# A mixture-of-experts kernel in Winograd form: second-layer products in alternating groups of two

## The chip, the core and the metric

One NeuronCore of a Trainium2 chip runs the whole program. The metric is device time in microseconds (us) of one execution, median of several runs.

## The reference, cut to what matters

```python
x = attention(q, packed(k, v, p))             # 4 batches x 576 tokens, 8 heads of 64
x = moe_ref(x, w_in, w_out)                   # h = x @ w_in; (h * cos(h)) @ w_out
P = sinkhorn(exp(x @ w_gate))                 # 2304 tokens, 8 experts
out = np.zeros((N, D))
for e in range(E):                            # 8 experts, 512 -> 1024 -> 512
    h = np.maximum(x @ w1[e], 0.0)
    out += P[:, e:e + 1] * (h @ w2[e])
```

All of it is fp32. The change concerns the last loop, which takes nearly four fifths of the time.

## The kernel before, in words

The first part (attention, then the cosine layer) runs for about 390 us from orders written out by hand; the change leaves it alone except for the last few operations that prepare the second part.

The expert part is split into 16 units (half an expert each, `u` from 4 to 19) of three steps (`j`, 768 tokens each), so 48 steps. A step computes a first layer (x times w1, called G1 here, matmuls on line 758) and the second layer (h times w2, G2, line 849) of the step before. Each layer is a 2 by 2 block product in Winograd's form: seven products instead of eight, of 12 matmuls with 384 columns each (three matmuls per fp32 product, from a high and a low part of both factors). So a step has 14 products. The names `m` in `MULTS`, `WIDE` and `NARROW` number the products.

All eight PSUM banks are one tile, `bank`. G1 works in two pairs of banks, X and Y (`two_banks`), which exchange their parts from step to step; G2 accumulates its seven products in two chains, in banks 4, 5 and 6, 7 (`WIDE`), or, while bank 7 is needed for the gate's logits and normalisation or for output tiles, in banks 4, 5 and 6 alone (`NARROW`). The engines beside TensorE do the rest:

- ScalarE (ACT) makes copies between the bank pairs and casts the high parts: L741 of h, L710 of w1, L242 of w2, L665 of x.
- VectorE (DVE) makes the low parts of h (L742), adds G2's sums into the accumulator `acc` (L869), applies relu and the gate's scale (L770), and forms the sums of h (L813, L828, L831).
- GpSimd (POOL) makes the low parts of the weights and their sums (L711, L714, L243, L246).
- SyncE issues all loads.

The order on each engine is the order in which the Python code issues (`manual_schedule`); a queue is served strictly from its front. In the loop over `n` a step issues, seven times, one G1 product, an evacuation, one split of an h sum (`h_steps`), and one G2 product (`g2_step`):

```python
for n in range(7):
    step_side()
    next(steps)                  # G1 product n
    if prev is not None:
        h_steps(s - 1, n + 7)    # split of an h sum
    ...
    next(steps)                  # its evacuation
    if prev is not None:
        g2_step(*prev, n, narrow, pair_no)
```

`step_side` issues the gate's logits (L928, L932, L935) and its normalisation piece by piece in the first steps. In the first unit the slots of x are computed on the way (`x_steps`); later they are loaded, four slots in turn. `w1_make` and `t_make` are generators whose steps prepare the weights of the next unit. `scale_first` (L907) multiplies the accumulator by the first expert's gate once, in three steps of the third unit. `out_tile` (L913 to L916) transposes finished tiles in a bank, copies them out and stores them.

Of the kernel before, what the change touches and what calls it, by code (L numbers as in the profile page):

```python
# [8 lines left out]
F32 = mybir.dt.float32  # L9
# [5 lines left out]
ALU = mybir.AluOpType  # L15
# [19 lines left out]
MULTS = (0, 5, 1, 6, 4, 3, 2)  # L35
# [69 lines left out]
def tile_kernel(ctx: ExitStack, tc: tile.TileContext, qT, kT, v, pT, w_in, w_out, w_gate, w1, w2, out):  # L105
# [129 lines left out]
    def t_make(u):  # L235
# [13 lines left out]
        put(1, b11)  # L249
        yield  # L250
        comb(b11, b12, b11)
        put(5, b11)
        yield
        comb(b11, b22, b11)
        put(6, b11)
        yield
        put(3, b22)
        yield
        comb(b12, b22, b12)
        put(7, b12)  # L260
        yield
        put(2, b21)
        yield
        comb(b21, b21, b11)
# [425 lines left out]
    def w1_make(u, places):  # L690
# [28 lines left out]
        yield  # L719
        comb(s2, s1, a11, ALU.subtract)  # L720
        put(5, s2)
        yield
        put(1, a12)
        yield
        comb(a11, a11, a21, ALU.subtract)
        put(6, a11)
        yield
        comb(a12, a12, s2, ALU.subtract)
        put(4, s1)
# [44 lines left out]
    def g1_steps(u, j):  # L774
        s = NJ * u + j
        x = counts["chunk"] % 2
        counts["chunk"] += 1
        X, Y = two_banks(x), two_banks(1 - x)
        r22, r11, r21, r12, rs = (halves(t) for t in (raws[s % 2], *raws[2:6]))
        b = halves(base)  # L780

        g1_mult(u, 0, x, True)
        if u == U1 and j == 0:
            wh = w_slot(w1_slots[u][0])[0]
            for p in range(2):
                nc.tensor.matmul(
                    bank[:, 2 * (1 - x) + p, 0:HT], lhsT=wh[:, 0, 0:P], rhs=x_slot(0)[0][:, 0, :],
                    start=True, stop=True, skip_group_check=True,
                )
        yield  # L790
        nc.scalar.copy(Y, X)  # L791
        yield
        g1_mult(u, 5, 1 - x, False)
        yield
        nc.scalar.copy(b, Y)
        yield
        g1_mult(u, 1, x, False)
        yield
        relu_scaled(u, j, r22, X, 0)
        yield  # L800
        g1_mult(u, 6, 1 - x, False)
        yield
        nc.scalar.copy(X, Y)
        nc.vector.tensor_tensor(out=b, in0=b, in1=Y, op=ALU.subtract)
        yield
        g1_mult(u, 4, x, False)
        yield
        relu_scaled(u, j, r11, X, 1)
        yield
        g1_mult(u, 3, 1 - x, False)  # L810
        yield
        relu_scaled(u, j, r21, Y, 0)
        nc.vector.tensor_tensor(out=rs, in0=r21, in1=r22, op=ALU.add)  # L813
        nc.gpsimd.tensor_tensor(out=r21, in0=r11, in1=r21, op=ALU.subtract)  # L814
        yield
        g1_mult(u, 2, x, False)
        yield
        nc.vector.tensor_tensor(out=X, in0=X, in1=b, op=ALU.add)  # L818
        relu_scaled(u, j, r12, X, 1)
        yield  # L820

    def h_steps(s, n):
        r22, r11, r21, r12, rs = (halves(t) for t in (raws[s % 2], *raws[2:6]))
        if n == 6:
            h_split(s, 1, r11)
        elif n == 7:
            h_split(s, 5, rs)
            nc.vector.tensor_tensor(out=rs, in0=rs, in1=r11, op=ALU.subtract)  # L828
        elif n == 8:
            h_split(s, 6, rs)  # L830
            nc.vector.tensor_tensor(out=rs, in0=r12, in1=rs, op=ALU.subtract)  # L831
        elif n == 9:
            h_split(s, 3, rs)
        elif n == 10:
            h_split(s, 7, r21)
        elif n == 11:
            h_split(s, 2, r12)
        elif n == 12:
            h_split(s, 4, r22)
# [19 lines left out]
    def g2_add(j, r, d, banks, tiles):  # L859
# [22 lines left out]
        ((1, 0, BOTH, True, ((1, 1),)),), ((5, 1, (0,), True, ((2, 2), (1, 2))),),  # L882
        ((6, 0, BOTH, False, ((1, 2),)), (5, 1, (1,), True, ((2, 2), (1, 2)))),
        ((3, 1, (0,), True, ((1, 2),)),),
        ((7, 0, BOTH, False, ((2, 2),)), (3, 1, (1,), True, ((1, 2),))),
        ((2, 1, (0,), True, ((1, 1),)),),
        ((4, 0, BOTH, False, ((2, 1),)), (2, 1, (1,), True, ((1, 1),))),
    )

    def g2_step(u, j, n, narrow, pair_no):  # L890
        sets = ((4, 5), (6, 6)) if narrow else ((4, 5), (6, 7))
        if pair_no and not narrow:
            sets = sets[::-1]
        for m, chain, tiles, start, outs in (NARROW if narrow else WIDE)[n]:
            g2_mult(u, j, m, sets[chain], tiles, start)
            for r, d in outs:
                g2_add(j, r, d, sets[chain], tiles)
# [5 lines left out]
    def scale_first(j):  # L903
        for th in range(2):
            block = acc_cols(2 * HT * j + HT * th, HT)
            scale = pb[j][:, HT * th:HT * th + HT].unsqueeze(1).to_broadcast([P, KD, HT])
            nc.vector.tensor_tensor(out=block, in0=block, in1=scale, op=ALU.mult)  # L907
# [96 lines left out]
    with tc.manual_schedule():  # L1004
# [138 lines left out]
        def x_steps(n, tmp, end=7 * NJ):  # L1143
            if n < end:
                x_sum(n, tmp)
# [153 lines left out]
```

## Time and profile before

| what | value |
|---|---|
| median of 3 runs (lowest to highest) | 1870.76 us (1870.05 to 1871.47) |
| profiled execution: time, span | 1870.89 us, 1868.9 us |
| TensorE busy, share of span | 1825.5 us, 98% |
| VectorE busy, share | 1449.8 us, 78% |
| ScalarE, GpSimd busy, share | 827.1 us, 44%; 774.1 us, 41% |
| matmuls | 11753, of which 8064 in the 672 products of the expert part |
| mean granted TensorE clock | 0.996 of 2.4 GHz |

The span runs from the first to the last instruction; the profiled execution's own time is 2.0 us longer. A matmul's shown duration (about 337 ns) is longer than the distance to the next one's start (about 173 ns), since matmuls are pipelined: what a matmul costs is read from the starts. Idle time in brackets is counted from a modelled end, so the starts are used for that as well.

### The profile page before, as it was taken

Reading aid. Unit: us, or ns where it says so; the run is one execution under the profiler, and the core shown is the slowest. Engines: PE = TensorE matmul, PEld = TensorE weight load, DVE = VectorE, ACT = ScalarE, POOL = GpSimd, SP = SyncE. Lnnn points to the kernel's source line nnn. Section 1 sums busy time; section 2 is a strip of 40 time slices with the busy share of each in tenths; the row PEclk is TensorE's granted clock in tenths of the full one; section 3 lists DMA queues with packets and bytes.
Section 4 is the critical chain, followed back from the end, with each engine's and each line's share of the span. In section 5 each row is a group of like instructions: output and inputs, shape, how many; then the busy total and the mean of one; then the engine's idle time right before and its main releaser. Section 6 shows DMA issues by size and latency. Waiting matters only on the chain.

```text
span 1868.9 us, 29782 instructions
## 1 busy us (share of the span) xinstructions
PE 1825.5 (98%) x11753; PEld 1776.9 (95%) x11753; DVE 1449.8 (78%) x1614; ACT 827.1 (44%) x1248; POOL 774.1 (41%) x542
## 2 busy tenths in 40 slices
PE   7999999999999999999999999999999999999998
PEld 4799999988999899999999999999999999999998
DVE  5877777558887888777878787878787877877876
ACT  5877787656544242333333233333333324333333
POOL 3545555453434443444444434434434443443420
PEclk9999999999999999999999999999999999999999
DMA  8511111034766576666766666676766766666662
GB/s 284 186 47 46 55 48 58 9 136 175 234 194 225 188 229 217 226 209 208 226 217 209 216 218 224 201 235 209 229 210 217 225 210 209 216 228 209 212 196 100
DMA packets 220839, 345.20 MB, mean 185 GB/s; under 512 B 13836, under 2 KB 190748, under 8 KB 220700
## 3 DMA queue, kind: packets, MB, share of 16 engines
q1 hardware_dynamic: 220700, 343.29, 56.2%
q8 instruction: 94, 1.54, 0.3%
q14 instruction: 45, 0.37, 0.1%
HBM read 321.93 MB, written 21.31 MB: 184 GB/s over the span
## 4 chain that ended last, share of the span: by engine, by line
PE 70%; POOL 9%; issue 9%; DVE 7%; ACT 4%; DMA 1%; SPq 0%; POOLq 0%; ACTq 0%; DVEq 0%
PE bank L758 27%; PE bank L849 25%; PE bank L606 11%; POOL tlo L243 4%; POOL raw L246 3%; PE bank L547 2%; DVE hreg L742 2%; PE bank L549 2%; PE bank L548 2%; POOL raw L814 2%; DVE bank L818 1%; DVE raw L770 1%; DVE acc L907 1%; ACT bank L791 1%; PE bank L483 1%
## 5 line engine op out<-in xcount | busy, mean ns | idle before, releaser
L849 PE MATMUL bank<-hreg,thi 128*128 128x384 f32 x2016 | 518.2, 337 | 12.3 <-DVE hreg L742 5.1
L758 PE MATMUL bank<-xh 128*128 128x384 f32 x1344 | 458.9, 341 | 5.1 <-ACT bank L791 5.0
L758 PE MATMUL bank<-xh,xl 128*128 128x384 f32 x1344 | 453.5, 337 | 0.0
L758 PE MATMUL bank<-xl,xh 128*128 128x384 f32 x1344 | 453.4, 337 | 0.0
L869 DVE TENSOR_TENSOR acc<-bank,acc 128x768 f32<-128x768 f32 (+1 forms) x351 | 317.1, 906 | 150.3 <-PE bank L849 146.7
L849 PEld LDWEIGHTS bank<-hreg,thi 128*128 128x128 f32 x2016 | 366.9, 188 | 15.3 <-DVE hreg L742 6.3
L742 DVE TENSOR_TENSOR hreg<-raw,hreg 128x768 fp32r<-128x768 f32 x252 | 313.8, 1245 | 49.7 <-ACT hreg L741 48.2
L849 PE MATMUL bank<-hreg,tlo 128*128 128x384 f32 x1008 | 340.4, 338 | 0.0
L711 POOL TENSOR_TENSOR xl<-wraw,xh 128x512 fp32r<-128x512 f32 x112 | 159.6, 1430 | 337.6 <-ACT xh L710 337.6
L741 ACT CAST hreg<-raw 128x768 fp32r<-128x768 f32 x252 | 209.7, 836 | 139.4 <-DVE raw L770 44.9
L758 PEld LDWEIGHTS bank<-xh 128*128 128x128 f32 x1344 | 252.7, 188 | 14.8 <-ACT bank L791 10.1
L758 PEld LDWEIGHTS bank<-xl,xh 128*128 128x128 f32 x1344 | 253.4, 189 | 0.0
L758 PEld LDWEIGHTS bank<-xh,xl 128*128 128x128 f32 x1344 | 253.2, 188 | 0.0
L243 POOL TENSOR_TENSOR tlo<-raw,thi 128x512 fp32r<-128x512 f32 x112 | 157.7, 1419 | 208.2 <-ACT thi L242 208.2
L814 POOL TENSOR_TENSOR raw<-raw,raw 128x768 f32<-128x768 f32 x48 | 89.4, 1862 | 315.7 <-DVE raw L813 315.7
L849 PEld LDWEIGHTS bank<-hreg,tlo 128*128 128x128 f32 x1008 | 189.4, 188 | 0.0
L606 PE MATMUL bank<-hreg,whi 128*128 128x288 f32 x1024 | 187.9, 295 | 0.2 <-DVE rbuf L587 0.2
L849 PE MATMUL bank<-slot,thi 128*128 128x384 f32 x672 | 172.2, 337 | 0.1
L770 DVE SCALAR_TENSOR_TENSOR raw<-bank,pb 128x768 f32<-128x768 f32 x168 | 160.0, 952 | 13.4 <-PE bank L758 12.0
L606 PEld LDWEIGHTS bank<-hreg,whi 128*128 128x128 f32 x1024 | 153.2, 188 | 2.1 <-DVE rbuf L587 1.2
L242 ACT CAST thi<-raw 128x512 fp32r<-128x512 f32 x112 | 69.6, 621 | 191.5 <-POOL raw L246 191.5
L563 POOL TENSOR_TENSOR hreg<-rbuf,hreg 128x576 fp32r<-128x576 f32 x64 | 91.9, 1439 | 97.4 <-ACT hreg L557 89.8
(150 smaller groups left out, 2643.9 us busy)
## 6 DMA issues: line engine op xcount, KB each, us to landing
xh<-xd SPq DMA_DIRECT2D x315, 384.0 KB, 3.3
xl<-xd SPq DMA_DIRECT2D x315, 384.0 KB, 3.9
raw<-w SPq DMA_DIRECT2D x32, 512.0 KB, 6.2
wraw<-w SPq DMA_DIRECT2D x30, 512.0 KB, 5.9
pb<-pd SPq DMA_DIRECT2D x24, 384.0 KB, 4.5
raw<-w_in SPq DMA_DIRECT2D x16, 512.0 KB, 4.4
raw<-w_out SPq DMA_DIRECT2D x16, 512.0 KB, 3.7
xd<-xh SPq DMA_DIRECT2D x21, 384.0 KB, 3.1
```

Of the source, the lines that this page charges most:

```text
L242: nc.scalar.copy(hi, src)
L243: nc.gpsimd.tensor_tensor(out=lo, in0=src, in1=hi.bitcast(F32), op=ALU.subtract)
L563: nc.gpsimd.tensor_tensor(out=lo, in0=r, in1=hi.bitcast(F32), op=ALU.subtract)
L606: nc.tensor.matmul(ps[:, di, 0:HC], lhsT=lhsT, rhs=rhs, start=(n in (0, 6)), stop=(n in (17, 23)),)
L711: nc.gpsimd.tensor_tensor(out=lo, in0=src, in1=hi.bitcast(F32), op=ALU.subtract)
L741: nc.scalar.copy(hi, src)
L742: nc.vector.tensor_tensor(out=lo, in0=src, in1=hi.bitcast(F32), op=ALU.subtract)
L758: nc.tensor.matmul(dst, lhsT=w, rhs=t[:, k, :], start=start and k == 0 and w is a and t is th, stop=k == 1 and w is bq, skip_group_check=True,
L770: nc.vector.scalar_tensor_tensor(out=out, in0=src, scalar=0.0, in1=scale, op0=ALU.max, op1=ALU.mult)
L814: nc.gpsimd.tensor_tensor(out=r21, in0=r11, in1=r21, op=ALU.subtract)
L849: nc.tensor.matmul(dst, lhsT=w, rhs=t[:, p, :], start=start and p == 0 and w is a and t is hh, stop=p == 1 and w is bq, skip_group_check=True,
L869: nc.vector.tensor_tensor(out=dst, in0=src, in1=dst, op=ALU.add)
```

## The change

The loop over `n` becomes a loop over `k` with four groups: two G1 products (one in the last group), then two G2 products (one in the last). G1's products come in the order 0, 6, 1, 5, 4, 3, 2. Product 6 is evacuated at once into `base` with its sign turned (`neg`), and the sum of products 0 and 6 is made in PSUM, so that 5 accumulates on it. The splits of h are issued at other places. The first expert's scaling is cut into four pieces per step, one behind each group. w2's combinations are issued one generator step earlier, with the product that is done with their input. The narrow form is used for one step less. Behind the last step the seven products of G2 are issued in the order 1, 2, 5, 6, 3, 7, 4, over three pairs of banks, with output tiles between them.

```diff
-MULTS = (0, 5, 1, 6, 4, 3, 2)
+MULTS = (0, 6, 1, 5, 4, 3, 2)
...
         yield
         put(1, b11)
-        yield
         comb(b11, b12, b11)
+        yield
         put(5, b11)
...
+    def g1_group(u, j, k, x):
+        r22, r11, r21, r12, rs = step_tiles(NJ * u + j)
+        X, Y, neg = two_banks(x), two_banks(1 - x), halves(base)
+        if k == 0:
+            g1_mult(u, 0, x, True)
+            nc.scalar.copy(r22, X)
+            g1_mult(u, 6, 1 - x, True)
+            nc.scalar.activation(neg, Y, AF.Copy, bias=0.0, scale=-1.0)
+            nc.vector.tensor_tensor(out=Y, in0=Y, in1=r22, op=ALU.add)
+        elif k == 1:
+            g1_mult(u, 1, x, False)
+            relu_scaled(u, j, r22, X, 0)
+            g1_mult(u, 5, 1 - x, False)
+            nc.scalar.copy(X, Y)
+        elif k == 2:
+            g1_mult(u, 4, x, False)
+            relu_scaled(u, j, r11, X, 1)
+            g1_mult(u, 3, 1 - x, False)
+        else:
+            g1_mult(u, 2, x, False)
+            nc.vector.tensor_tensor(out=X, in0=X, in1=neg, op=ALU.add)
+            relu_scaled(u, j, r12, X, 1)
...
     WIDE = (
-        ((1, 0, BOTH, True, ((1, 1),)),), ((5, 1, BOTH, True, ((2, 2),)),),
-        ((6, 0, BOTH, False, ((1, 2),)),), ((3, 1, BOTH, False, ((1, 2),)),),
-        ((7, 0, BOTH, False, ((2, 2),)),), ((2, 1, BOTH, True, ((1, 1),)),),
+        ((1, 0, BOTH, True, ((1, 1),)), (5, 1, BOTH, True, ((2, 2),))),
+        ((6, 0, BOTH, False, ((1, 2),)), (3, 1, BOTH, False, ((1, 2),))),
+        ((7, 0, BOTH, False, ((2, 2),)), (2, 1, BOTH, True, ((1, 1),))),
         ((4, 0, BOTH, False, ((2, 1),)),),
     )
...
+    def scale_first(j, k):
+        r, d = k // 2 + 1, k % 2 + 1
+        scale = pb[j][:, HT * (2 - r):HT * (3 - r)].unsqueeze(1).to_broadcast([P, 2, HT])
+        block = out_block(j, r, d)
+        nc.vector.tensor_tensor(out=block, in0=block, in1=scale, op=ALU.mult)
...
-                narrow = s <= NJ * U1 + 5 or s == NJ * NU - 1
+                narrow = s <= NJ * U1 + 4 or s == NJ * NU - 1
...
+                for k in range(4):
                     step_side()
+                    if prev is not None:
+                        if k == 0:
+                            split_h(s - 1, 5)
+                            second_sum(s - 1)
+                        elif k == 1:
+                            third_sum(s - 1)
+                    g1_group(u, j, k, x)
+                    if prev is not None and k == 2:
+                        split_h(s - 1, 4)
+                    if k == 2:
+                        first_sums(u, j, x)
+                    if prev is not None and k == 1:
+                        split_h(s - 1, 3)
+                    step_side()
                     if prev is not None:
+                        for n, part in enumerate((NARROW if narrow else WIDE)[k]):
+                            g2_part(*prev, part, banks)
+                            if n == 0:
+                                if k == 0:
+                                    split_h(s - 1, 6)
+                                elif k == 1:
+                                    split_h(s - 1, 7)
+                                    split_h(s - 1, 2)
+                                elif k == 2:
+                                    split_h(s, 1)
...
+                    if s == NJ * NU - 1 and k < 3:
+                        out_tile(0, 2 * k, 7)
+                        out_tile(0, 2 * k + 1, 7)
```

What this does to two queues is seen in the built programs' orders. The first place is ACT's queue in one step of the wide form. COPY bank<-bank is the copy between bank pairs behind a G1 product (line 803 before, 790 now). CAST hreg or slot is the high half of an h sum. `raw_4410` before, `raw_4411` now, is `rs`, which holds the sums for products 5, 6 and 3 one after the other; `raw_4408` and `raw_4409` are `r21` (product 7) and `r12` (product 2) before, `raw_4409` and `raw_4410` now. Before:

```order
746 L741 CAST hreg<-raw_4410 128x768
747 L791 COPY bank<-bank 128x2x384
748 L741 CAST hreg<-raw_4410 128x768
749 L795 COPY base<-bank 128x768
750 L710 CAST xh<-wraw 128x2x256
751 L741 CAST hreg<-raw_4410 128x768
752 L710 CAST xh<-wraw 128x2x256
753 L741 CAST slot<-raw_4408 128x768
754 L803 COPY bank<-bank 128x2x384
755 L710 CAST xh<-wraw 128x2x256
756 L741 CAST hreg<-raw_4409 128x768
```

Now:

```order
711 L741 CAST hreg<-raw_4411 128x768
712 L782 COPY raw_4000<-bank 128x768
713 L784 ACTIVATE base<-bank 128x768
714 L741 CAST hreg<-raw_4411 128x768
715 L242 CAST thi<-raw_8121 128x512
716 L790 COPY bank<-bank 128x2x384
717 L741 CAST slot<-raw_4411 128x768
718 L741 CAST hreg<-raw_4409 128x768
719 L741 CAST hreg<-raw_4410 128x768
```

The third cast of `rs`, for product 3, stood ahead of the copy on line 803, with two casts between them; now it stands right behind the copy on line 790.

The second place is DVE's queue where the first expert's result is scaled. Before:

```order
586 L869 TENSOR_TENSOR acc_1628<-bank,acc_1628 128x384
587 L907 TENSOR_TENSOR acc_101<-acc_101,pb_3997 128x4x384 x2
588 L742 TENSOR_TENSOR hreg<-raw_4407,hreg 128x768
589 L818 TENSOR_TENSOR bank<-bank,base 128x2x384
590 L869 TENSOR_TENSOR acc_101<-bank,acc_101 128x2x384
```

Now, one piece of 768 elements at a time (line 882), four in a step:

```order
596 L847 TENSOR_TENSOR acc_1628<-bank,acc_1628 128x2x384
597 L882 TENSOR_TENSOR acc_1628<-acc_1628,pb_3998 128x2x384
598 L812 TENSOR_TENSOR raw_4411<-raw_4410,raw_4411 128x768
599 L770 SCALAR_TENSOR_TENSOR raw_4000<-bank,pb_3997 128x768
600 L742 TENSOR_TENSOR hreg<-raw_4411,hreg 128x768
601 L847 TENSOR_TENSOR acc_1628<-bank,acc_1628 128x2x384
```

Two multiplications of 1536 elements that stood together, ahead of a split and of sums that TensorE waits for, stand apart now, each behind an addition of G2.

## Rows read from the trace of the kernel before

**Rows 1.** The page, busy time by engine over the whole span.

```profile
PE 1825.5 (98%) x11753; PEld 1776.9 (95%) x11753; DVE 1449.8 (78%) x1614; ACT 827.1 (44%) x1248; POOL 774.1 (41%) x542
```

**Rows 2.** Windows: stretch, its length, PE PEld DVE ACT POOL busy, clock, DMA.

```profile
400.00:450.00 50.00, 44.65 (x272) 40.69 (x271) 36.88 (x40) 28.17 (x44) 23.67 (x15) 0.97 0.46 163
...
550.00:600.00 50.00, 47.51 (x264) 46.96 (x262) 39.31 (x39) 20.56 (x30) 21.16 (x14) 0.97 0.69 225
...
1000.00:1050.00 50.00, 50.00 (x287) 50.00 (x286) 40.98 (x40) 17.01 (x25) 19.87 (x14) 1.00 0.65 209
```

**Rows 3.** Waits of TensorE, 400 to 700 us: total, times, longest.

```profile
PE bank L935 <- ACT l_sb L932: 4.4, 1, 4.4
PE bank L849 <- ACT acc L871: 3.4, 2, 1.8
```

**Rows 4.** The same view, 700 to 1840 us.

```profile
PE bank L758 <- ACT bank L791: 3.6, 13, 0.3
```

**Rows 5.** Timeline of TensorE: two G2 products behind each other, 12 and 6 matmuls.

```profile
551.07 0.51 PE L849 MATMUL bank<-hreg,thi 128*128 128x384 f32 x2
...
553.17 0.51 PE L849 MATMUL bank<-hreg,thi 128*128 128x384 f32 x2
...
554.21 0.38 PE L984 MATMUL bank<-ident,by_e 128*72 128x128 f32 x2
```

**Rows 6.** Timeline: a G2 product between two of G1, first matmul and the next product's.

```profile
1002.24 0.51 PE L849 MATMUL bank<-hreg,thi 128*128 128x384 f32 x2
...
1004.35 0.34 PE L758 MATMUL bank<-xh 128*128 128x384 f32 x1
```

**Rows 7.** Timeline around a wait that comes once in a unit (ACT, then TensorE).

```profile
1066.54 0.62 ACT L242 CAST thi<-raw 128x512 fp32r<-128x512 f32 x1 [10.28 <-POOL raw L246]
...
1071.54 0.34 PE L849 MATMUL bank<-hreg,tlo 128*128 128x384 f32 x1
1072.14 0.44 PE L758 MATMUL bank<-xh 128*128 128x384 f32 x1 [0.26 <-ACT bank L791]
1072.42 0.34 PE L758 MATMUL bank<-xl,xh 128*128 128x384 f32 x1
```

**Rows 8.** Timeline where the first expert is scaled: TensorE's waits and DVE.

```profile
588.71 0.58 PE L849 MATMUL bank<-hreg,thi 128*128 128x384 f32 x2 [2.49 <-DVE acc L869]
...
646.78 5.30 DVE L907 TENSOR_TENSOR acc<-acc,pb 128x1536 f32<-128x1536 f32 x2
...
654.10 0.45 PE L849 MATMUL bank<-hreg,thi 128*128 128x384 f32 x1 [1.75 <-DVE hreg L742]
...
656.84 0.44 PE L758 MATMUL bank<-xh 128*128 128x384 f32 x1 [0.55 <-ACT bank L791]
```

**Rows 9.** Timeline of TensorE in the first unit.

```profile
422.22 0.55 PE L935 MATMUL bank<-ident,l_sb 128*128 128x128 f32 x3 [4.37 <-ACT l_sb L932]
```

**Rows 10.** Timeline: the links of a split, from a product's end to TensorE.

```profile
1082.73 0.51 PE L849 MATMUL bank<-hreg,thi 128*128 128x384 f32 x2
1082.93 0.78 ACT L803 COPY bank<-bank 128x768 f32<-128x768 f32 x1 [3.50 <-PE bank L758]
1083.62 0.84 ACT L741 CAST slot<-raw 128x768 fp32r<-128x768 f32 x1
...
588.45 0.82 ACT L741 CAST slot<-raw 128x768 fp32r<-128x768 f32 x1
589.31 0.96 DVE L742 TENSOR_TENSOR slot<-raw,slot 128x768 fp32r<-128x768 f32 x1 [0.28 <-ACT slot L741]
...
532.81 0.94 DVE L742 TENSOR_TENSOR hreg<-raw,hreg 128x768 fp32r<-128x768 f32 x1
533.81 0.44 PE L849 MATMUL bank<-hreg,thi 128*128 128x384 f32 x1 [0.75 <-DVE hreg L742]
```

**Rows 11.** The page's group of L742: count, busy, mean ns.

```profile
L742 DVE TENSOR_TENSOR hreg<-raw,hreg 128x768 fp32r<-128x768 f32 x252 | 313.8, 1245 | 49.7 <-ACT hreg L741 48.2
```

**Rows 12.** Timeline of TensorE at the end: the transposes behind the last product.

```profile
1860.32 1.47 PE L913 MATMUL bank<-ident,acc 128*128 128x128 f32 x12
```

More of the change, by code (lines that the diff above doesn't have):

```diff
@@ L249, in t_make @@
         put(1, b11)
+        comb(b11, b12, b11)
         yield
[L251 removed]
         put(5, b11)
+        comb(b11, b22, b11)
         yield
[L254 removed]
         put(6, b11)
@@ L772, in relu_scaled @@
             )
[L774 to L812, printed above, removed]
@@ L881, in tile_kernel, with g2_part @@
     NARROW = (
[L882 to L887, printed above, removed]
-    )
[L890 to L897, printed above, removed]
+        ((1, 0, BOTH, True, ((1, 1),)), (5, 1, (0,), True, ((2, 2), (1, 2)))),
+        ((5, 1, (1,), True, ((2, 2), (1, 2))), (6, 0, BOTH, False, ((1, 2),)),
+         (3, 1, (0,), True, ((1, 2),))),
+        ((3, 1, (1,), True, ((1, 2),)), (7, 0, BOTH, False, ((2, 2),)),
+         (2, 1, (0,), True, ((1, 1),))),
+        ((2, 1, (1,), True, ((1, 1),)), (4, 0, BOTH, False, ((2, 1),))),
+    )
+    def g2_part(u, j, part, banks):
+        m, chain, tiles, start, outs = part
+        g2_mult(u, j, m, banks[chain], tiles, start)
+        for r, d in outs:
+            g2_add(j, r, d, banks[chain], tiles)
     def pb_load(e, j):
@@ L1196, in tile_kernel @@
                 first_unit = u == U1
-                narrow = s <= NJ * U1 + 5 or s == NJ * NU - 1
-                steps = g1_steps(u, j)
-                for n in range(7):
+                narrow = s <= NJ * U1 + 4 or s == NJ * NU - 1
+                banks = ((4, 5), (6, 6)) if narrow else ((4, 5), (6, 7))
+                if pair_no and not narrow:
+                    banks = banks[::-1]
+                x = counts["chunk"] % 2
+                counts["chunk"] += 1
+                for k in range(4):
@@ L1212, in tile_kernel @@
-                    if first_unit and 7 * j + n + 3 < 7 * NJ + 2:
-                        x_steps(7 * j + n + 5, [halves(t) for t in pb])
-                    if s == NJ * NU - 1 and n < 6:
-                        out_tile(0, n, 7)
-                    if first_unit and j == 0 and n < 3:
-                        next(preps[u], None)
-                    if 7 * j + n in range(1, 8):
+                        if k == 0:
[3 more added lines that the diff above has]
+                            third_sum(s - 1)
@@ new lines, in tile_kernel @@
+                    for n in range(2 * k, min(2 * k + 2, 7)):
+                        if first_unit and 7 * j + n + 3 < 7 * NJ + 2:
+                            x_steps(7 * j + n + 5, [halves(t) for t in pb])
+                    if s == NJ * NU - 1 and k < 3:
+                        out_tile(0, 2 * k, 7)
+                        out_tile(0, 2 * k + 1, 7)
+                    if first_unit and j == 0:
+                        for _ in range((2, 1, 0, 0)[k]):
+                            next(preps[u], None)
```

158 lines of the change are left out of this document (86 added, 72 removed).

## The prediction

> **What bounds the kernel now.** First the busy times: TensorE is busy for 1825.5 of 1868.9 us [rows 1], so a change can gain only what TensorE waits, or what its products take beyond their pace. Then the windows, to see where it is not full: 44.65 of 50 us in the opening of the expert part, 47.51 where the first expert is scaled, all of 50 in the steady part [rows 2]. The mean granted clock is 0.97 in the first two windows: part of each ran at the lower of the two levels (1.2 GHz), which cost 0.03 x 50 = 1.5 us in each; in the first it came behind a wait of 4.37 us [rows 9]. Then TensorE's waits, which name the releaser: the logits' copy and copies into the accumulator early on [rows 3], and from 700 us on one kind alone, 13 times [rows 4]. Last, the timeline, for what one wait costs from start to start. I work against the profiled execution's 1870.89 us; the median of the runs is 1870.76, so the two are 0.13 apart. A difference under 0.2% (3.7 us) I call no change.
>
> **Part 1, fewer changes between the two layers.** A G2 product between two of G1 takes 1004.35 - 1002.24 = 2.11 us [rows 6]. Where two G2 products follow each other, the first 12 matmuls take 2.10 and the next six 1.04 us [rows 5]: the six run at 0.173 each, and twelve at that pace would take 2.08. So a product that follows another layer pays about 0.026 us at its start, and one that follows its own layer, by this row, nothing. A step has 14 such changes now and will have 8. That is 47 steps (the first has no second layer) x 6 x 0.026 = **-7.3 us**. The bounds are 0 and 47 x 6 x 0.03 = 8.5. The row with nothing to pay is a product whose h had been waited for before, so the upper end is not safe, but it is the nearest row.
>
> [...]
>
> **Part 2, the wait once in a unit.** From 1071.54 to 1072.14 is 0.60 us where 0.173 is the pace, and the next start comes 0.28 later instead of 0.173 [rows 7]: 0.43 + 0.11 = 0.54, 13 times [rows 4]: **-7.0 us**. Its cause is ACT's queue, which had stood for 10.28 us behind a sum of w2's on GpSimd [rows 7], so that a split, then DVE, then the copy X to Y came late; the copy has only the 2.1 us of one G2 product. Now that sum is issued a generator step earlier, and the copy of product 0 need not be done before a product two slots later. I find nothing in its place: the last relu of a step (sum on DVE, then relu, 0.95 each) must be done 4.2 us behind product 2. Bounds -7.0 and 0.
>
> **Part 3, scaling the first expert.** Two multiplications of 1536 elements hold DVE for 5.30 us in one go, and TensorE then waits 2.49, or 1.75 and once more 0.55 [rows 8]. The first of the three steps loses 2.49, 1.5 of clock [rows 2] and about 0.2 of restart; the other two 1.75 + 0.55 + 0.25 each: 4.2 + 5.1 = 9.3. In pieces of about 1 us behind a G2 sum the same work fits: 23 operations of DVE of 0.95 and four more make 26 us of a step of 30, and each piece ends before the next relu is due. I take all of it, **-9.3 us**; the bounds are -9.3 and -4 (if one wait in each step stays).
>
> **Part 4, the opening.** The two waits on accumulator copies, 3.4 us in all [rows 3], go: the next product in those banks comes 4.2 us later instead of 2.1. The wait for the logits' copy, 4.4 us [rows 3] with its 1.5 of clock, was caused by ACT's queue, which holds x's casts and w2's casts that wait for GpSimd. It holds them still; following the queue through the first step I get three waits of about 0.8, 0.6 and 1.6 us instead, so 5.9 becomes 3.0. Two warm-up matmuls (L786) go, 0.35. Together **-6.7 us**, bounds 0 and -9.7.
>
> **Part 5, the end.** From the last product's end to the span's end it is 1868.9 - 1860.32 = 8.6 us [rows 12]. Three tiles instead of six now stand behind the last product, which gains some 2 us, and the last step sends two tiles through bank 7 one right behind the other, three times, which costs a copy's wait of about 0.9 each. I take **0**, bounds -4 and +3.
>
> **Part 6, a new wait.** This one speaks against the change. In group k=1 G1 issues products 1 and 5, then the copy X from Y; the cast of `rs` for product 3 stands right behind that copy in ACT's queue. G2 then runs product 6 and product 3. Count from the first matmul of product 6, which is the slot behind product 5. A copy begins 0.20 behind such a start, the cast 0.69 behind the copy (1082.73, 1082.93, 1083.62), DVE's low half 0.86 behind the cast (588.45, 589.31), and TensorE starts 1.00 behind that (532.81, 533.81) [rows 10]: 0.20 + 0.69 + 0.86 + 1.00 = 2.75. The low half is wanted by the second matmul of product 3, at 2.11 + 0.17 = 2.28. So TensorE waits 0.47, and the restart costs 0.11 as in part 2 but saves 0.02 of a start: 0.56 us. Before the change this cast stood ahead of the copy and had a product more of time. In the narrow form half of product 5 stands in between, so only the 42 wide steps pay: 42 x 0.56 = **+23.5 us**. Bounds: 0, if the links overlap more than the rows say, and +36 with the mean of L742 (1.245 us [rows 11] for 0.94). I take the links one by one, since each was seen with nothing else in its way; by the order of issue GpSimd has nothing to do at that moment. Behind the waiting matmul stand the rest of product 3 and G1's next group, which all move by the same amount. The other splits have 4 us and more: product 5's is issued two slots ahead, those of 6, 7, 2, 4 and 1 a whole group.
>
> Loads: x's products are loaded by the same four slots, 14.7 us ahead as before, since a slot is free as long as four products of G1 and the G2 products between them take.
>
> **Sum:** -7.3 - 7.0 - 9.3 - 6.7 + 0 + 23.5 = -6.8, so 1870.9 - 6.8 = **1864.1 us**. The likeliest case by itself reaches from 1857 to 1871.
>
> **Rivals.**
> A start costs by product, not by change of layer. For it: every product in the steady part takes the same 2.11 us, and only half a product speaks against it. Then part 1 is 0: 1871.4 us. [...] Chance 0.17.
>
> GpSimd falls beside the split of product 3 (slower). The place is L742 of product 3; the price is the difference between the mean of L742 and one alone, 1.245 - 0.94 = 0.30 us [rows 10, 11], 42 times, +12.8: 1876.9 us. It decides from 0.25 us a step on (10.5 us over 42 steps, which is 6.8 + 3.7). For it: ACT and GpSimd share weights' work whose time depends on loads; against: in the order of issue, that work is queued behind this split in group 1 and done by then in group 0. The Trainium skill (SBUF — State Buffer, section "Who interferes with whom") has a two-input VectorE operation and a GpSimd one shut each other out for a whole instruction, so one meeting could cost more than this mean; no run here shows it at this place. Chance 0.16.
>
> The new wait isn't there (faster): a link of part 6 is shorter or overlaps. Then 1864.1 - 23.5 = 1840.6 us. Against it: the four links each stand in a row. Chance 0.10.
>
> The opening and the scaling give nothing (waits of other names take their place, since DVE and ACT are as full as before): +6.7 + 5.3 gives 1876. Chance 0.07. That the change doesn't group the products is excluded by the built order.
>
> **How the numbers follow.** The forecast has 0.50. Of it three quarters lie under 1867.1 and nearly all the rest within 3.7 us; with the case without the new wait, faster has 0.375 + 0.10 = 0.48. Within 0.2% lie the rest of the forecast's and the start cost by product: 0.12 + 0.17 = 0.29. Slower: GpSimd beside the split, the empty opening: 0.16 + 0.07 = 0.23. The range leaves out the case without the new wait and the far ends of the slower ones: 1853 to 1878. Its lower end is the forecast with parts 1, 4 and 5 at their bounds (-1.2, -3.0, -4) and a link of part 6 shorter by 0.07 (-3); its upper end is 1 us above the GpSimd case.
>
> **What would show it.** Among TensorE's waits a line for L742, some 40 times, about 0.4 us each, that was not there after 700 us [part 6]; the line of L791 with its 13 gone [part 2]; steps of 29.9 us where they were 29.5 (14 x 2.11) and every third 0.54 longer; products that follow their own layer at 2.08 us [part 1]; clock 1.00 in the window from 550 to 600 us [part 3]. A steady part without waits on L742 would make part 6 and the forecast wrong by up to 23 us; waits there of 1 us would make it wrong on the other side.

## The result and the profile of the changed kernel

The changed kernel takes 1896.99 us (median of 4 runs, 1892.60 to 1898.76) where the kernel before, on the same chip, takes 1870.40. The ratio is 1.0138, with a 95% interval from 1.0120 to 1.0157. So it is slower by 26.6 us, where 1864.1 was forecast and the range ended at 1878. The profiled execution took 1898.76 us, its span 1896.7.

To see where the time went, the program is cut at the first G1 matmul (line 758) of each step, in both traces, and the lengths are subtracted. Nothing of the change lies ahead of the first step; that column moves by 1 to 2 us from one execution to the next.

| against the profiled execution of before, us | ahead of step 1 | steps 1 to 4 | 5 to 9 | 10 to 47 | 48 and end | span |
|---|---|---|---|---|---|---|
| changed kernel | -0.2 | **+22.6** | -7.3 | +11.4 | +1.3 | +27.8 |

The forecast had these places at -6.7 for the opening, about -9 for the scaling (steps 7 to 9), +8.3 for steps 10 to 47 (38 steps with 0.56 more and 0.156 less, and the 7.0 of part 2), and 0 for the end. The second of part 4's two waits on accumulator copies lies in step 5 of the kernel before, and step 5 is 2.8 us shorter now (33.15 to 30.35), so the opening in the sense of part 4 is steps 1 to 5: +19.8. One place fails, and it fails by 26.5 us: the opening.

First the busy time of the changed kernel, which answers to [rows 1]: TensorE is busy longer, and yet for a smaller share.

```profile
PE 1833.8 (97%) x11751; PEld 1776.2 (94%) x11751; DVE 1469.0 (77%) x1614; ACT 823.3 (43%) x1247; POOL 847.7 (45%) x542
```

The windows, with the columns of [rows 2]:

```profile
400.00:450.00 50.00, 44.58 (x264) 39.15 (x264) 34.64 (x38) 29.28 (x46) 23.61 (x15) 0.93 0.41 144
450.00:500.00 50.00, 37.39 (x187) 35.11 (x186) 39.87 (x54) 23.29 (x35) 19.94 (x13) 0.91 0.54 179
500.00:550.00 50.00, 44.67 (x248) 44.29 (x247) 36.58 (x64) 21.82 (x32) 16.44 (x11) 0.95 0.51 165
550.00:600.00 50.00, 49.26 (x282) 48.59 (x281) 39.55 (x44) 22.29 (x33) 21.66 (x14) 1.00 0.70 235
1000.00:1050.00 50.00, 49.33 (x281) 48.69 (x280) 40.18 (x39) 18.12 (x26) 22.74 (x14) 1.00 0.64 206
```

Where the first expert is scaled, 550 to 600 us, TensorE is fuller than before (49.26 against 47.51) and the clock is whole. The steady part now has 49.33 of 50. But from 450 to 500 us TensorE is busy for 37.39 us only, and in all three early windows part of the time ran at the lower level of the clock: 0.07 + 0.09 + 0.05 of 50 us is 10.5 us, where the kernel before lost 1.5 there (0.97, 1.00, 1.00).

TensorE's waits from 400 to 700 us, the five largest, which answer to [rows 3]:

```profile
PE bank L827 <- DVE acc L847: 9.1, 4, 3.9
PE bank L758 <- DVE xl L670: 6.4, 3, 4.8
PE bank L916 <- ACT l_sb L913: 3.5, 2, 2.8
PE bank L932 <- DVE top L928: 2.7, 1, 2.7
PE bank L827 <- DVE hreg L742: 2.1, 4, 0.8
```

Of the 3.4 us on copies into the accumulator 0.4 is left, as forecast. The logits' copy is no better: 3.5 us in two waits, and 0.8 in a third on the logits' sum (L900), where 3.0 was expected for three. New in the opening are the first two lines, 15.5 us: G2 waits for additions into the accumulator (L847), and G1 for the low halves of x (L670). From 700 to 1840 us, which answers to [rows 4]:

```profile
PE bank L827 <- DVE hreg L742: 9.8, 29, 0.4
PE bank L827 <- DVE slot L742: 3.0, 9, 0.3
```

The 13 waits on L791 are gone, and 38 on L742 stand in their place, with four more between 560 and 700 us: 42, one in each wide step. Both are parts 2 and 6 of the prediction.

Part 1 is seen in the starts of four products that stand one behind the other, two of G2 and two of G1 (timeline of TensorE; the first matmul of each, and the first of the next group):

```profile
1001.00 0.52 PE L827 MATMUL bank<-hreg,thi 128*128 128x384 f32 x2
...
1003.10 0.51 PE L827 MATMUL bank<-hreg,thi 128*128 128x384 f32 x2
...
1005.18 0.34 PE L758 MATMUL bank<-xh 128*128 128x384 f32 x1
...
1007.28 0.33 PE L758 MATMUL bank<-xh 128*128 128x384 f32 x1
...
1009.36 0.51 PE L827 MATMUL bank<-slot,thi 128*128 128x384 f32 x2
```

The first product of a group takes 2.10, the second 2.08, in either layer. Over steps 11 to 47 the medians by place lie between 2.105 and 2.107 us for the first and between 2.080 and 2.083 for the second (product 3, with its wait, left out): a change of layer costs about 0.025 us, and a product behind its own layer does not pay it.

Part 6, in the next group of that step (ACT, DVE and TensorE):

```profile
1009.56 0.78 ACT L790 COPY bank<-bank 128x768 f32<-128x768 f32 x1 [6.06 <-PE bank L758]
...
1010.26 2.30 ACT L741 CAST hreg<-raw 128x768 fp32r<-128x768 f32 x3
...
1011.13 0.96 DVE L742 TENSOR_TENSOR hreg<-raw,hreg 128x768 fp32r<-128x768 f32 x1 [2.69 <-ACT hreg L741]
...
1011.47 0.34 PE L827 MATMUL bank<-hreg,thi 128*128 128x384 f32 x1
...
1012.14 0.44 PE L827 MATMUL bank<-hreg,thi 128*128 128x384 f32 x1 [0.34 <-DVE hreg L742]
1012.42 0.34 PE L827 MATMUL bank<-hreg,tlo 128*128 128x384 f32 x1
```

The four links from 1009.36 are 0.20 + 0.70 + 0.87 + 1.01 = 2.78, where 2.75 was forecast. The second matmul of product 3 starts 0.67 behind the first (0.17 is the pace) and the next 0.28 behind it: 0.50 + 0.11 = 0.61 us a step, where 0.58 had been worked out ahead of the 0.02 for a start.

Now the opening. From 480 us on VectorE's queue reads so, with three of TensorE's rows put in at their times:

```profile
480.03 0.31 DVE L954 SCALAR_TENSOR_TENSOR prob<-prob,rc 128x144 f32<-128x144 f32 x1
...
481.92 1.58 DVE L742 TENSOR_TENSOR hreg<-raw,hreg 128x768 fp32r<-128x768 f32 x1
483.43 2.03 DVE L742 TENSOR_TENSOR slot<-raw,slot 128x768 fp32r<-128x768 f32 x1
485.38 1.61 DVE L847 TENSOR_TENSOR acc<-bank,acc 128x768 f32<-128x768 f32 x2
486.90 0.95 DVE L670 TENSOR_TENSOR xl<-pb,xh 128x768 fp32r<-128x768 f32 x1
...
487.91 0.69 PE L758 MATMUL bank<-xl,xh 128*128 128x384 f32 x1 [4.75 <-DVE xl L670]
488.39 0.52 PE L758 MATMUL bank<-xh,xl 128*128 128x384 f32 x1
...
488.71 0.52 PE L758 MATMUL bank<-xh 128*128 128x384 f32 x1
```

A round of the gate's normalisation (L952 to L946, the first row is one of its eight operations), two splits and two sums of half a tile stand ahead of the low half of x that the second G1 product of the group wants. TensorE waits 4.75 us and then runs at the lower level (1.2 GHz): 0.32 us from start to start. Because G1 was late, the relu behind it is late, and the next rows follow:

```profile
491.51 0.82 ACT L767 ACTIVATE raw<-bank 128x768 f32<-128x768 f32 x1 [6.90 <-PE bank L758]
...
492.35 0.96 DVE L803 TENSOR_TENSOR raw<-raw,raw 128x768 f32<-128x768 f32 x1 [2.76 <-ACT raw L767]
...
493.23 0.16 DVE L952 TENSOR_SCALAR rc<-bank 128x8 f32<-128x8 f32 x1
493.39 1.83 POOL L804 TENSOR_TENSOR raw<-raw,raw 128x768 f32<-128x768 f32 x1 [8.75 <-DVE rc L952]
...
493.66 1.73 DVE L954 SCALAR_TENSOR_TENSOR prob<-prob,rc 128x144 f32<-128x144 f32 x1
...
497.22 0.41 DVE L946 TENSOR_REDUCE cs<-prob 128x8 f32<-128x144 f32 x1
497.55 0.55 DVE L847 TENSOR_TENSOR acc<-bank,acc 128x384 f32<-128x384 f32 x1
...
498.24 0.98 PE L827 MATMUL bank<-slot,thi 128*128 128x384 f32 x2 [3.39 <-DVE acc L847]
```

The next round, here 4.4 us long, stands directly ahead of the one addition for which bank 6 is not yet free, and TensorE waits again, for 3.39 us.

At the end two things stand against each other. In the last step two tiles one right behind the other go through bank 7:

```profile
1842.78 0.60 PE L887 MATMUL bank<-ident,acc 128*128 128x128 f32 x4
1844.06 0.66 PE L887 MATMUL bank<-ident,acc 128*128 128x128 f32 x4 [0.68 <-ACT rows L892]
...
1889.47 1.91 PE L887 MATMUL bank<-ident,acc 128*128 128x128 f32 x16
```

Of the 0.95 us from the last transpose of the first tile to the first of the second, some 0.9 is wait, and this happens three times. From the last product's end to the span's end it is 1896.7 - 1889.5 = 7.2 us instead of 8.6 [rows 12]. Together 2.7 - 1.4 = +1.3, as the table has it.

### The profile page after: what moved, and what is told of

Read it like the earlier page. It is cut to its first block, busy times and chain, and to the rows that moved or that the text cites. A ratio compares the mean times of both kernels' runs of the same rounds, so it can differ in the third digit from the quotient of the medians.

```text
span 1896.7 us, 29773 instructions
## 1 busy us (share of the span) xinstructions
PE 1833.8 (97%) x11751; PEld 1776.2 (94%) x11751; DVE 1469.0 (77%) x1614; ACT 823.3 (43%) x1247; POOL 847.7 (45%) x542
## 4 chain that ended last, share of the span: by engine, by line
PE 83%; DVE 8%; ACT 5%; issue 2%; DMA 1%; POOL 1%; SPq 0%; DVEq 0%; ACTq 0%; POOLq 0%
PE bank L758 35%; PE bank L827 30%; PE bank L606 10%; DVE hreg L742 3%; PE bank L547 2%; PE bank L548 2%; PE bank L549 2%; ACT hreg L741 2%; ACT bank L790 1%; DVE slot L742 1%; DVE acc L847 1%; PE bank L483 1%; DVE xl L670 1%; ACT slot L741 1%; DMA raw<-w_in 0%
## 5 line engine op out<-in xcount | busy, mean ns | idle before, releaser
L827 PE MATMUL bank<-hreg,thi 128*128 128x384 f32 x2016 | 527.0, 340 | 19.7 <-DVE hreg L742 11.9
L742 DVE TENSOR_TENSOR hreg<-raw,hreg 128x768 fp32r<-128x768 f32 x252 | 320.7, 1280 | 119.1 <-ACT hreg L741 119.1
L847 DVE TENSOR_TENSOR acc<-bank,acc 128x768 f32<-128x768 f32 (+1 forms) x344 | 314.8, 917 | 29.0 <-PE bank L827 23.9
L243 POOL TENSOR_TENSOR tlo<-raw,thi 128x512 fp32r<-128x512 f32 x112 | 176.3, 1579 | 297.5 <-ACT thi L242 277.7
L804 POOL TENSOR_TENSOR raw<-raw,raw 128x768 f32<-128x768 f32 x48 | 88.8, 1851 | 378.8 <-DVE raw L803 367.9
L741 ACT CAST hreg<-raw 128x768 fp32r<-128x768 f32 x252 | 204.2, 834 | 121.2 <-DVE raw L770 81.4
L711 POOL TENSOR_TENSOR xl<-wraw,xh 128x512 fp32r<-128x512 f32 x112 | 193.9, 1743 | 136.4 <-ACT xh L710 127.9
L770 DVE SCALAR_TENSOR_TENSOR raw<-bank,pb 128x768 f32<-128x768 f32 x168 | 160.3, 954 | 25.2 <-PE bank L758 21.2
L790 ACT COPY bank<-bank 128x768 f32<-128x768 f32 x48 | 37.6, 783 | 254.9 <-PE bank L758 249.1
```

The costliest lines, as they stand in the source:

```text
L243: nc.gpsimd.tensor_tensor(out=lo, in0=src, in1=hi.bitcast(F32), op=ALU.subtract)
L711: nc.gpsimd.tensor_tensor(out=lo, in0=src, in1=hi.bitcast(F32), op=ALU.subtract)
L741: nc.scalar.copy(hi, src)
L742: nc.vector.tensor_tensor(out=lo, in0=src, in1=hi.bitcast(F32), op=ALU.subtract)
L770: nc.vector.scalar_tensor_tensor(out=out, in0=src, scalar=0.0, in1=scale, op0=ALU.max, op1=ALU.mult)
L827: nc.tensor.matmul(dst, lhsT=w, rhs=t[:, p, :], start=start and p == 0 and w is a and t is hh, stop=p == 1 and w is bq, skip_group_check=True,
```

## Experiments

The theory after this reading: the steady part does what the forecast says, and what was missed is the opening, for two reasons on VectorE. The rounds of the normalisation, which `step_side` used to issue one piece per product, fall between the G1 and the G2 products of every group, right ahead of G2's sums; and the low halves of x are issued in pairs behind both G2 products. The rivals: the new product order or evacuation is dear in itself, or VectorE is too full there for any order of groups. The table of lengths, for all of what follows, and the first five steps one by one:

| profiled execution against that of before, us | ahead of step 1 | steps 1 to 4 | 5 to 9 | 10 to 47 | 48 and end | span |
|---|---|---|---|---|---|---|
| split of 3 early (1) | -1.4 | +23.7 | -11.9 | **-12.3** | +1.1 | -0.6 |
| x steps apart (2) | +0.7 | +17.7 | -8.9 | +11.2 | +1.1 | +21.8 |
| first unit not grouped (3) | -1.6 | **+2.2** | -5.0 | +11.3 | +1.2 | +8.1 |
| parts 2 and 3 on the kernel before (4) | -0.3 | -0.5 | -8.6 | -6.9 | 0.0 | -16.2 |
| normalisation ahead of G1 (5) | -1.1 | **+9.2** | -8.2 | +11.4 | +1.3 | +12.7 |
| (2) and (5) together (6) | +0.8 | +6.6 | -8.2 | +11.3 | +1.2 | +11.8 |
| (1), six steps not grouped (7) | -1.1 | -0.5 | -7.9 | -12.3 | +0.4 | -21.4 |
| (7), tiles apart (8) | -2.2 | -0.6 | -7.9 | -12.3 | **-2.2** | -25.2 |

| length of step, us | 1 | 2 | 3 | 4 | 5 |
|---|---|---|---|---|---|
| before | 34.56 | 33.71 | 34.47 | 30.50 | 33.15 |
| changed kernel | 35.19 | 37.84 | 45.39 | 37.40 | 30.35 |
| first unit not grouped (3) | 30.85 | 35.97 | 35.67 | 32.93 | 34.20 |
| parts 2 and 3 on the kernel before (4) | 30.86 | 35.94 | 35.38 | 30.53 | 32.32 |
| normalisation ahead of G1 (5) | 35.19 | 36.58 | 37.69 | 32.94 | 31.08 |
| (2) and (5) together (6) | 34.99 | 35.34 | 36.55 | 32.94 | 31.08 |
| (7) | 30.87 | 35.94 | 35.66 | 30.23 | 33.30 |

### 1. The split of product 3 ahead of the copy

```diff
             g1_mult(u, 5, 1 - x, False)
+            if NJ * u + j > NJ * U1:
+                split_h(NJ * u + j - 1, 3)
             nc.scalar.copy(X, Y)
...
-                    if prev is not None and k == 1:
-                        split_h(s - 1, 3)
```

> One edit to the changed kernel: the split of product 3 is issued ahead of the copy X from Y (line 790) instead of behind it. Theory (part 6 of the prediction): the wait of the second matmul of product 3 is the sum of four links, of which the copy is one; the trace of the changed kernel has 0.50 + 0.11 us of it in each wide step. Without the copy in the way the low half is ready 0.69 us earlier, 0.2 us before it is wanted: the waits on L742 (15.3 us, 43 times) go, a wide step takes 29.95 - 0.61 = 29.35 us, and the time falls by 42 x 0.61 = 25 us, to about 1872. Rival: the copy, now 0.8 us later, or the relu behind it, becomes what TensorE waits for, so that steps stay at 29.9 us or get a line for L790, and the time stays within 5 us of 1897.

Measured: 1869.67 us (10 runs), 0.9992 of before (0.9982 to 1.0002); against the changed kernel -27.3. Two of three wide steps take 29.32 us, the third 29.35. The waits of TensorE from 560 to 1800 us, all of them:

```profile
PE bank L829 <- DVE hreg L742: 0.5, 1, 0.5
PE bank L758 <- DVE raw L770: 0.3, 1, 0.3
PE bank L829 <- ACT hreg L741: 0.3, 1, 0.3
```

Of the 42 one is left, in step 8: there TensorE waits 0.3 us for the cast (L741) and then 0.5 for the low half, and on VectorE the sum that the cast needs stands behind a piece of the scaling. From 700 to 1800 us there is no wait at all. In steps 10 to 47 the difference goes from +11.4 to -12.3, 0.62 us for each of the 38. Where the low half now comes from (one wide step; the copy is line 792 here):

```profile
937.92 0.84 ACT L741 CAST hreg<-raw 128x768 fp32r<-128x768 f32 x1 [3.69 <-DVE raw L814]
...
938.84 1.02 DVE L742 TENSOR_TENSOR hreg<-raw,hreg 128x768 fp32r<-128x768 f32 x1
...
939.85 0.51 PE L829 MATMUL bank<-hreg,thi 128*128 128x384 f32 x2
940.04 0.78 ACT L792 COPY bank<-bank 128x768 f32<-128x768 f32 x1 [1.29 <-PE bank L758]
```

The cast does not wait for G1 at all, only for the sum on VectorE, so the low half is ready by 939.9 us, 2.3 us ahead of the matmul that wants it; my 0.2 was too careful. This settles part 6: its cause is the place of one cast behind one copy. It also shows part 1 by itself: 29.32 where a step of before takes 29.47 is 0.15, as forecast for six changes of layer (29.35 is 0.12).

### 2. The two x steps of a group apart

```diff
+                    x_next(2 * k)
                     step_side()
...
-                    for n in range(2 * k, min(2 * k + 2, 7)):
-                        if first_unit and 7 * j + n + 3 < 7 * NJ + 2:
-                            x_steps(7 * j + n + 5, [halves(t) for t in pb])
+                    x_next(2 * k + 1)
```

Here `x_next(n)` is the inner call of the lines that go, for one `n`.

> One edit to the changed kernel, first unit only: the two x steps of a group stand apart, one behind the G1 products and one behind the G2 products, instead of both behind the G2 products. Theory 1: the opening's 22.6 us come from x's low halves, which stand on VectorE behind the splits and sums of both G2 products and are wanted by the second G1 product at once. Then the waits of L758 on L670 (6.4 us) go, the queue gets shorter for what stands behind, the clock in the windows from 400 to 550 us comes back from 0.93, 0.91, 0.95, and some 12 to 18 us go: 1880 to 1885. Theory 2: VectorE's and ScalarE's queues are full with whatever order, because the narrow form with two G2 products in a row asks for its sums at once: the waits on L670 go but those on accumulator sums (L847, 9 us) and the normalisation (L928) grow, and the time stays over 1890.

Measured: 1891.51 us, 1.0112 of before (1.0097 to 1.0127); against the changed kernel -5.5. The waits on L670 are gone, but those on L847 have grown to 11.3 us, and one of 3.6 us on a copy into the accumulator is new. Steps 1 to 4 lose 4.9 us of their 22.6. So the place of x's low halves is a cause, and the smaller one; by the numbers it is the second theory that held, but for the wait on L928, which is gone and not longer.

### 3. The first unit not grouped

The three steps of the first unit in a loop over `n`: one G1 product, a split, its evacuation, then one G2 product in the narrow form of before; seven side steps a step. The product order and the evacuations are the changed ones, and all behind the first unit too.

```diff
+                for n in range(7) if first_unit else ():
+                    step_side()
+                    g1 = g1_single(u, j, n, x)
+                    next(g1)
+                    if prev is not None and n < 6:
+                        split_h(s - 1, H_ORDER[n])
...
+                        for part in SINGLE[n]:
+                            g2_part(*prev, part, banks)
...
-                for k in range(4):
+                for k in () if first_unit else range(4):
```

> The changed kernel with the first unit (three steps) issued one G1 product, one G2 product in turn, as before, and its side steps, splits and x steps in the places they had before; product order, evacuation and everything behind the first unit are those of the changed kernel. Theory: grouping in the first unit is what costs the opening. The first three steps return to the lengths of the kernel before (34.6, 33.7, 34.5 us instead of 35.2, 37.8, 45.4), which is 15.7 us, and the fourth, still grouped and narrow, gives some of its 6.9 us: 1897 - 16 to 22 = 1875 to 1881. Rival: the new order of products or the evacuation through a negative copy costs the opening, grouped or not: the three steps stay over 112 us together (they were 102.7 before, 118.4 after), and the time stays above 1890.

Measured: 1879.22 us, 1.0048 of before (1.0033 to 1.0063); against the changed kernel -17.8. The three steps take 102.5 us together where before has 102.7. The gain in step 1 (30.85 us for 34.56) is not the product order's: experiment 4, which keeps the old order and has w2's combinations early as well, has 30.86 there and 102.2 for the three. So the product order and the evacuation through a negative copy cost next to nothing (0.3 us over three steps), and the rival falls: it is the grouped order. The clock is 1.00, 1.00 and 0.97 in the three early windows.

### 4. Parts 2 and 3 alone, on the kernel before

```diff
         put(1, b11)
-        yield
         comb(b11, b12, b11)
+        yield
         put(5, b11)
...
-                    if NJ * (U1 + 1) + 2 <= s < NJ * (U1 + 2) + 2 and n == 5:
+                    if NJ * (U1 + 1) + 2 <= s < NJ * (U1 + 2) + 2 and n > 2:
                         i = s - NJ * (U1 + 1) - 2
-                        scale_first(i)
-                        pb_load(1, i)
+                        scale_first(i, n - 3)
+                        if n == 6:
+                            pb_load(1, i)
```

> The kernel before with two parts of the change alone: w2's combinations one generator step earlier (part 2) and the first expert's scaling in four pieces, one behind each of the last four G2 products of its step (part 3). Theory: both parts are independent of the grouping: the 13 waits on L791 go (0.54 each, -7.0), and the three scaling steps lose their waits of 1.75 to 2.5 us and the lower clock (-9.3): 1870.4 - 16.3 = 1854. Rival: the waits on L791 also come from the rest of the order of two products one behind the other, and the pieces, one per product instead of one per group, make the splits behind them late: less than 8 us go, above 1862.

Measured: 1854.77 us, 0.9915 of before (0.9900 to 0.9930), that is -16.2. From step 10 on it is -6.9 with all 13 waits gone, where -7.0 was forecast for part 2. The three steps in which TensorE waits for the scaling (7 to 9; its operations are issued in steps 6 to 8, from the last step of the second unit on) give -4.0, -1.3 and -2.4, together -7.8 of the -9.3 of part 3. Neither part needs the groups.

Part 2 does something more here: with w2's combinations early the wait of 4.4 us on the logits' copy is gone and step 1 takes 30.86 us instead of 34.56. That agrees with the prediction's cause for it, ACT's queue held up by w2's casts. Steps 2 and 3 give most of the gain back (35.94 and 35.38 us instead of 33.71 and 34.47); what holds them was not tried.

### 5. The normalisation's rounds ahead of G1

```diff
         nc.scalar.activation(prob, lg, AF.Exp, bias=nmx, scale=1.0)
         yield
+        yield
```

With two side steps in a group and rounds that take two, one empty step moves all eight rounds from the place between G1 and G2 to the place ahead of G1.

> One edit to the changed kernel: one empty side step more ahead of the gate's normalisation, so that each of its rounds (nine small operations on VectorE, about 3.5 us) stands ahead of a group's G1 products instead of between them and the G2 products. Theory: in the grouped order these rounds always fall right ahead of a group's G2 sums, and the narrow form takes its one bank again one product later; the trace of the changed kernel has the two longest waits of L827 on L847 (3.6 and 4.1 us) directly behind such rounds. Then these two go, with some of the lower clock: 8 to 11 us, 1886 to 1889. Rival: VectorE is full in the first unit wherever the rounds stand; now the splits of products 5 and 3 or x's low halves come late instead, and the time stays over 1893.

Measured: 1883.49 us, 1.0072 of before (1.0057 to 1.0087); against the changed kernel -13.5, more than expected. Steps 3 and 4 take 37.69 and 32.94 us instead of 45.39 and 37.40. TensorE's waits from 400 to 560 us:

```profile
PE bank L916 <- ACT l_sb L913: 3.5, 2, 2.8
PE bank L758 <- DVE xl L670: 3.5, 3, 2.2
PE bank L827 <- ACT acc L849: 2.6, 2, 2.2
PE bank L827 <- DVE acc L847: 2.1, 2, 1.1
```

L847 falls from 9.1 to 2.1 us, and L670 from 6.4 to 3.5 although x's steps were not touched: the round had stood ahead of them as well. The clock's three windows are 0.93, 0.97 and 1.00, which is 5.5 us of the 13.5. One line, with nothing taken away, gives back half of the loss.

### 6. Both edits of the opening

The edits of 2 and 5 together.

> Both edits of the opening together, x's steps apart and the normalisation's rounds ahead of G1, in the changed kernel, everything still grouped. Theory: the two causes are separate and add: 1891.5 less 8 to 11 is 1880 to 1883, about where the first unit without groups stands (1879.2), and the waits on L847 in the opening are under 5 us together. Rival: the grouped narrow form itself, which takes bank 6 for three half products in a group, keeps its waits on L847: over 8 us of them stay and the time is over 1887.

Measured: 1881.01 us, 1.0062 of before (1.0047 to 1.0077); against the changed kernel -16.0. The waits on L847 are 3.3 us. The total is as expected, but the two do not quite add (5.5 + 13.5 = 19.0): with the rounds out of the way x's place is worth 2.5. Of the 22.6 us in the first four steps 6.6 stay, among them 4.2 us of waits on copies into the accumulator and 3.2 on the logits' copy. What orders those was not tried, so the cause of the 6.6 us stays open.

### 7. The early split, and six steps not grouped

The edit of 1, and the loop over `n` of 3 for the first two units (`u < U1 + 2`), narrow up to the sixth step.

> The changed kernel with the split of product 3 ahead of the copy, and with the first six steps (all of the narrow ones but the last) issued one product of each layer in turn as before; grouped from the seventh on. Theory: the opening then costs what it did before, and the rest what the run with the early split showed: 1870.7 - 0.5 in the first four steps, - 10 in the five with the first expert's scaling, - 12.3 in the steps behind them, + 1.2 at the end = 1849, between 1846 and 1852. Rival: the early waits come back in the steps where the order goes over from the one to the other, or the opening's new order of products costs as much as in the run with one such unit (+ 2.2 and more): above 1853, no better than the two small parts alone (1854.8).

Measured: 1850.12 us, 0.9895 of before (0.9879 to 0.9912). The first four steps cost what they cost before (-0.5), and steps 10 to 47 give the -12.3 of experiment 1. No wait appears where the order goes over. In the sum of the expectation the five steps of the scaling were put at -10 and gave -7.9.

### 8. And the last step's tiles apart

```diff
                     step_side()
+                    if s == NJ * NU - 1 and k < 3:
+                        out_tile(0, 2 * k, 7)
                     if prev is not None:
...
                     if s == NJ * NU - 1 and k < 3:
-                        out_tile(0, 2 * k, 7)
                         out_tile(0, 2 * k + 1, 7)
```

> The same, and in the last step of the loop the two output tiles of a group stand apart, one ahead of the G2 products and one behind them. Theory (part 5 of the prediction): two tiles through bank 7 one right behind the other cost a copy's wait of 0.9 us, three times; apart, the copy has a group of products to be done in, so 2.7 us go: 1846, and the three waits of L887's line on L892 in the last step are not there. Rival: the first tile then waits for the copy of the tile before it or holds ScalarE's queue ahead of a split, and less than 1 us goes.

Measured: 1847.40 us, 0.9878 of before (0.9863 to 0.9892). From the start of step 48 to the end it is 2.6 us less than in 7 (2.7 by the medians), as expected, and from 700 us to the end this is all that TensorE waits for:

```profile
PE bank L829 <- DVE acc L849: 0.2, 1, 0.2
```

This version is 22.9 us faster than the kernel before and 49.6 faster than the changed one. It keeps the groups where they bring something, from the seventh step on.

## Why the prediction was wrong

The step that failed is **part 4**, "following the queue through the first step I get three waits". The queue was followed through one step of the five that the opening takes. In that step the normalisation is not yet at work; it begins in step 2, its rounds run in steps 3 to 5, and there the groups put each round directly ahead of G2's sums and x's low halves. Measured: +22.6 us in steps 1 to 4, +19.8 with step 5, where the sum had -6.7. Of the 22.6, experiment 3 gives 20.4 back by taking the groups out of three steps, and experiment 5 gives 13.4 back by the place of the rounds alone. Even the first step was off: its waits from start to start are 0.9, 2.9 and 1.1 us, not 0.8, 0.6 and 1.6. Nor did the text reckon with clock behind new waits: in this trace each of the five waits of 2.7 to 4.8 us in the opening has a stretch at the lower level beside it, 10.5 us in three windows, and the three waits that the sum put into the first step carried none.

The term that came out in part 4, the accumulator copies (0.4 us left of 3.4), is not shown to be right in its reason, "the next product in those banks comes 4.2 us later". Where the other waits are eased the same copies hold TensorE again with the groups in place: 3.6 us in experiment 2, 2.6 in 5 and 4.2 in 6.

The rival "the opening and the scaling give nothing" named the right mechanism for the opening (waits of other names, since VectorE and ScalarE are as full as before), but its price ended at 0: it took the gain away and asked for no loss. For the scaling it did not hold: that gave 7.8 of its 9.3 us in experiment 4. The rival that was slower had its place elsewhere: GpSimd beside the split of product 3 does not show: the L742 that TensorE waits for takes 0.96 us in all 42 steps.

The other terms, by their measured sizes:

- **Part 1**, -7.3 forecast: steps 10 to 47 give -12.3 in experiment 1 and -6.9 by part 2 alone in experiment 4, so 5.4 us for 38 steps, 0.14 a step; for 47 steps that is -6.7. The rival that a start costs by product falls, 2.08 against 2.10.
- **Part 2**, -7.0 forecast: -6.9, alone in experiment 4.
- **Part 3**, -9.3 forecast: -7.8. In the three steps of experiment 4 four waits of 0.2 to 0.7 us stay, 1.7 in all from start to start.
- **Part 5**, 0 forecast: +1.3, the three waits in bank 7 being 0.9 each as said and the tail 1.4 instead of 2 us shorter.
- **Part 6**, +23.5 forecast: 42 x 0.61 = +25.6. The sum of four links was right to 0.03 us.

With +19.8 for -6.7 in steps 1 to 5, +25.6 for +23.5, -7.8 for -9.3, +1.3 for 0 and -6.7 for -7.3, the sum of -6.8 becomes about +25; the spans differ by 27.8. Most of what is left lies in step 8, the second of the scaling steps, where the groups have a longer wait of their own. Three rows of the changed kernel (VectorE, ScalarE, TensorE):

```profile
645.80 0.94 DVE L882 TENSOR_TENSOR acc<-acc,pb 128x768 f32<-128x768 f32 x1
...
648.57 0.78 ACT L790 COPY bank<-bank 128x768 f32<-128x768 f32 x1 [5.73 <-DVE raw L770]
...
650.15 0.45 PE L827 MATMUL bank<-hreg,thi 128*128 128x384 f32 x1 [1.40 <-ACT hreg L741]
```

A piece of the scaling stands ahead of a sum and a relu on VectorE, the copy waits for the relu, and the cast of product 3 stands behind the copy; so TensorE waits 1.4 us for the cast (experiments 2, 3, 5 and 6 show the same wait). Part 3 had each piece end before the next relu is due; here it does not. That the piece is the cause is read from the order of the queue; no run shows it alone. Behind this wait the execution ran 50 us at a mean clock of 0.97, which is 1.5 us more.

## What to carry to other kernels

When an order is written in larger groups, look at everything that used to be issued once per product: it now falls at one fixed place in the group, and in a queue that is served from its front that place may be just ahead of what TensorE waits for. Follow the queues through every step in which a side computation runs, not through the first alone, and price a failure there with the clock beside the waits (here 10.5 us in three windows). A wait whose links each stand in a row could be forecast here to 0.03 us, and then it is better moved away than accepted: one cast put ahead of one copy was worth 27.3 us, more than parts 1, 2 and 3 gained together (21.4).

## What the runs showed of the hardware

In these rows a small operation of VectorE is held up beside GpSimd as a long one is. L954, on 144 elements, takes 0.31 us at 480.03 with GpSimd idle, and 1.73 us at 493.66, beside GpSimd's L804 of 1.83 us, which began 0.27 us earlier and ended 0.17 us ahead of it; a split of 768 elements (L742) takes 0.96 us at 1011.13 and 2.03 at 483.43, beside GpSimd's L711. The Trainium skill (SBUF — State Buffer, section "Who interferes with whom") has the two engines share one pair of SBUF ports under an exclusive lock, and a VectorE instruction with two SBUF inputs contend there with a GpSimd instruction that reads SBUF; these rows agree. The eight operations of a round (the expectation of experiment 5 counts nine) take 2.4 us from 479.60, most of it with GpSimd idle, and 4.4 us from 493.23.

A change of the layer that feeds TensorE costs about 0.025 us at the first product behind it: 2.105 to 2.107 against 2.080 to 2.083 us for twelve matmuls (medians over steps 11 to 47 of the changed kernel). What causes it no run here shows.
